# Weight conversion from a byte-shifted second load, earlier q, k and v loads, and MLP work beside the last regrouping

## Chip, cores, metric

One core of a Trainium2 chip. The metric is the device time of one execution in microseconds (us); medians of all runs of a kernel are quoted. Engines: PE is TensorE, DVE is VectorE, ACT is ScalarE, POOL is GpSimd, SP is SyncE.

## The reference, cut

```python
# q, k, v: (8, 8, 576, 64) float32; tau = 0.02
scores = np.matmul(q, k.transpose(0, 1, 3, 2)) / np.sqrt(64)
thresh = np.max(scores, axis=-1, keepdims=True) - tau
scores = np.where(scores >= thresh, scores, -1e9)
attn   = softmax(scores)                        # cut: written out in the reference
x      = (attn @ v)                             # -> (B*S, H*D) = (4608, 512)
h      = x @ w_in                               # w_in (512, 2048), float64 values
out    = (0.5 * h * (1 + erf(h / sqrt(2)))) @ w_out   # w_out (2048, 512), float64 values
```

The weights come as 64-bit floats; the kernel rebuilds 32-bit floats from their words.

## The kernel before

The attention works on 32 head pairs of 5 slots each (slot n = 5p + i). A slot computes scores, takes the softmax, and transposes the result into `pd`. Once a pair, the softmax weights are regrouped through DRAM: eight writes (`pd`), four more for the tail (`pd_tail`), two reads (`pT`). The MLP runs in the same slots from n = 24 on, filled in by `fill`. The weights come in 32 pieces of 128x512, loaded by `load_piece` and converted step by step by `conversions`, mostly before slot n = 26; that stretch is here called the front. (`sc` are the scores, `xT` the attention output before it is turned into `x`, `hT` the MLP's hidden layer.)

```python
xg = ctx.enter_context(tc.tile_pool(name="xg", bufs=6))   # weight pieces and x blocks
...
def load_piece():
    ...
    raw = xg.tile([P, 2 * PIECE], U32, tag="x", name="raw")
    nc.sync.dma_start(raw, src.bitcast(U32))
    raws.append((dst, raw))

def conversions():
    vec = nc.vector
    while raws:
        dst, raw = raws.pop(0)
        word = raw.rearrange("p (f w) -> p f w", w=2)
        lo, hi = word[:, :, 0], word[:, :, 1]
        ...
        nc.scalar.activation(low, lo, AF.Copy, bias=0.0, scale=2.0 ** -52)
        vec.tensor_scalar(cut, hi, 3, 0x3FFFFFF8, op0=ALU.logical_shift_left, op1=ALU.bitwise_and)
        yield 450
        vec.scalar_tensor_tensor(cut, hi, 0xC0000000, cut, op0=ALU.bitwise_and, op1=ALU.bitwise_or)
        yield 720
        vec.tensor_scalar(rest, hi, 27, 0xF, op0=ALU.logical_shift_right, op1=ALU.bitwise_and)
        yield 450
        vec.scalar_tensor_tensor(cut.bitcast(FP32), rest, 7.0, cut.bitcast(FP32), op0=ALU.is_ge, op1=ALU.mult)
        yield 720
        vec.tensor_scalar(two, cut, 0xFF800000, None, op0=ALU.bitwise_and)
        nc.gpsimd.tensor_tensor(low, low, two.bitcast(FP32), op=ALU.mult)
        nc.gpsimd.tensor_tensor(dst, low, cut.bitcast(FP32), op=ALU.add)
        load_piece()                  # the load three pieces on is asked for here
        converted[0] += 1
        yield 450
...
load(0, nc.scalar)
for _ in range(3):
    load_piece()
load(1)
turn_qk(0)
...
for n in range(len(slots) + WEIGH + 1):
    p, i = divmod(n, SLOTS)
    ...                               # scores, softmax, turn_p (pd at i = 4, pd_tail at i = 0)
    if i == 0 and p:
        fetch_p(p - 1)                # pT
    if i == 1 and p + 1 < NP and p:
        load(p + 1)                   # q, k: 4 DMAs each; v: 8
    if i == 2 and p + 1 < NP:
        turn_qk(p + 1)
    if n < BATCH + WEIGH:
        convert(3050)                 # so many ns of conversion steps in this slot
    elif batch < 2:
        convert(9000)
    if n > BATCH + WEIGH and batch < B:
        fill(...)                     # MLP work
    if i == WEIGH and p:
        weigh_v(p - 1)                # xT, then x
```

Nearly every DMA is issued by SyncE, in the order of the program.

## Time and profile before

| | before |
|---|---|
| median of 3 runs | 1647.19 us (1647.08 to 1648.49) |
| profiled execution | 1656.56 us, span 1654.7, mean PE clock 0.935 |
| PE, DVE, ACT, GpSimd busy, of the span | 87%, 60%, 36%, 6% |
| weight conversion on DVE, per piece | 420 + 1312 + 916 + 691 + 424 ns |
| slot n = 26 begins (PE bounds from here on) | 292.0 us |

How to read the views: a row of groups has line, engine, operation, output<-input, shape and count, then busy us and the mean ns of one, then the idle time just before them and what ended it. A row of a timeline has start, duration, engine, line and operation, and in brackets the wait. The granted clock is PE's clock as a share of full speed. In the view of groups by form of the kernel before, two conversion operations stand out:

```profile
L149 DVE SCALAR_TENSOR_TENSOR cut<-raw,cut 128x512 uint32<-128x512 uint32 x32 | 42.0, 1312 | 0.9
L152 DVE TENSOR_SCALAR rest<-raw 128x512 uint32<-128x512 uint32 x32 | 29.3, 916 | 0.0
```

The excess lies beside GpSimd's work: in the trace of the kernel before, those that overlap a GpSimd operation take 1595 and 1482 ns on average, the others 688 and 416.

### The profile page before, as it was taken

To read this page: it belongs to the slowest core of one execution; us is meant where nothing else is said; L and a number is where in the kernel's file an instruction comes from. 1 tells how busy PE (TensorE), PEld (TensorE's weight loads), DVE (VectorE), ACT (ScalarE), POOL (GpSimd) and SP (SyncE) were. 2 spreads that over 40 slices of the span, in tenths; PEclk is the share of its full clock that TensorE was granted. 3 is DMA by queue.
4 is the path that set the end of the run, shared out by engine and by line. 5 is a ranking of instruction groups with operands and counts; after the bars stand their busy time and mean duration, and the time that the engine had idled before them with its cause. 6 is when DMAs were issued, how large, how long until landed. Compare 5 with 4: busy or idle time off the path is not lost.

```text
span 1654.7 us, 17315 instructions
## 1 busy us (share of the span) xinstructions
PE 1434.5 (87%) x5888; PEld 888.9 (54%) x5888; DVE 993.3 (60%) x2176; ACT 592.0 (36%) x844; POOL 92.4 (6%) x77
## 2 busy tenths in 40 slices
PE   2334444999999999998999999999999998699999
PEld 1212223656565665656665655565657473456765
DVE  6988888776766766765766675676666675000000
ACT  3333322535354543442543344343535251101100
POOL 2232234000000000000000000000000000000000
PEclk9965556999999999999999999999999999799999
DMA  5656684576666666666576565666666665300000
GB/s 132 180 150 193 180 221 116 146 181 169 180 176 176 172 182 154 181 165 173 145 185 170 158 167 151 173 180 175 169 177 168 176 178 153 104 13 7 7 13 13
DMA packets 434982, 244.43 MB, mean 148 GB/s; under 512 B 245968, under 2 KB 418000, under 8 KB 426704
## 3 DMA queue, kind: packets, MB, share of 16 engines
q1 hardware_dynamic: 432528, 243.04, 55.9%
q8 instruction: 47, 0.77, 0.2%
q10 hardware_dynamic: 2368, 0.30, 0.1%
q14 instruction: 39, 0.32, 0.1%
HBM read 139.46 MB, written 103.81 MB: 147 GB/s over the span
## 4 chain that ended last, share of the span: by engine, by line
PE 66%; SPq 12%; DVE 12%; DMA 5%; ACT 2%; issue 2%; DVEq 0%; ACTq 0%
PE o_ps L341 27%; PE hT L330 24%; PE sc L224 9%; SPq L188 8%; PE xT L302 7%; DVE nmx L235 2%; DVE cut L149 2%; DMA turned<-pd_tail 2%; DVE p L249 2%; SPq L281 2%; SPq L277 1%; DMA k<-in_k_dram 1%; DVE rest L152 1%; DVE cut L154 1%; ACT p L236 1%
## 5 line engine op out<-in xcount | busy, mean ns | idle before, releaser
L330 PE MATMUL hT<-x,w_in 128*128 128x256 f32 x2304 | 526.0, 386 | 3.0 <-ACT x L313 3.0
L341 PE MATMUL o_ps<-w_out,g 128*128 128x512 f32 x1152 | 513.4, 597 | 0.0
L330 PEld LDWEIGHTS hT<-x,w_in 128*128 128x128 f32 x2304 | 439.4, 193 | 91.7 <-issue 26.8
L341 PEld LDWEIGHTS o_ps<-w_out,g 128*128 128x128 f32 x1152 | 214.5, 190 | 258.5 <-issue 255.4
L236 ACT ACTIVATE p<-sc,nmx 128x576 f32<-128x576 f32 x288 | 202.8, 740 | 419.6 <-DVE nmx L235 419.3
L235 DVE TENSOR_REDUCE nmx<-sc 128x1 f32<-128x576 f32 x288 | 206.1, 752 | 191.0 <-PE sc L224 190.0
L224 PE MATMUL sc<-kT,qT 64*128 64x288 f32 x1024 | 198.8, 477 | 134.9 <-DVE p L249 124.4
L224 PEld LDWEIGHTS sc<-kT,qT 64*128 64x128 f32 x1024 | 111.4, 207 | 229.9 <-issue 201.7
L249 DVE SCALAR_TENSOR_TENSOR p<-sc,thr,p 128x576 f32<-128x576 f32 x288 | 219.2, 792 | 0.3 <-ACT p L236 0.2
L302 PE MATMUL xT<-pT,v 128*64 128x288 f32 x1280 | 178.6, 434 | 34.7 <-DMA pT<-turned 20.9
L272 DVE STREAM_TRANSPOSE pd<-p 128x576 f32<-128x576 f32 x256 | 185.0, 756 | 8.9 <-DMA turned<-pd 8.9
L302 PEld LDWEIGHTS xT<-pT,v 128*64 128x64 f32 x1280 | 98.4, 145 | 117.1 <-issue 44.7
L334 ACT ACTIVATE g<-hT 128x512 f32<-128x512 f32 x144 | 84.2, 597 | 125.8 <-PE hT L330 125.0
L206 DVE STREAM_TRANSPOSE kT<-k 128x576 f32<-128x576 f32 x32 | 24.9, 778 | 167.3 <-DMA k<-in_k_dram 163.9
L260 DVE TENSOR_SCALAR p<-p,rden 128x576 f32<-128x576 f32 x252 | 121.0, 518 | 4.9
L334 ACT ACT_TABLE_LOAD x74 | 94.9, 1283 | 12.4 <-PE hT L330 11.4
L236 ACT ACT_TABLE_LOAD x73 | 93.7, 1283 | 1.3
L207 ACT ACTIVATE q<-q,q_scale 128x576 f32<-128x576 f32 x32 | 24.8, 774 | 183.8 <-DMA q<-in_q_dram 183.8
L224 PE MATMUL sc<-kT,q_tail 128*128 128x288 f32 x128 | 46.2, 490 | 43.8 <-DVE p L249 43.7
L344 ACT COPY o_sb<-o_ps 128x512 f32<-128x512 f32 x36 | 21.0, 582 | 138.8 <-PE o_ps L341 138.1
L313 ACT COPY x<-xT 128x256 f32<-128x256 f32 (+7 forms) x128 | 28.3, 288 | 90.8 <-PE xT L302 90.8
L224 PEld LDWEIGHTS sc<-kT,q_tail 128*128 128x128 f32 x128 | 25.1, 218 | 64.0 <-issue 57.2
(30 smaller groups left out, 439.9 us busy)
## 6 DMA issues: line engine op xcount, KB each, us to landing
pT<-turned SPq DMA_DIRECT2D x64, 1440.0 KB, 8.2
turned<-pd SPq DMA_DIRECT2D x256, 320.0 KB, 5.2
turned<-pd_tail SPq DMA_DIRECT2D x128, 80.0 KB, 3.0
q<-in_q_dram SPq DMA_DIRECT2D x128, 72.0 KB, 9.1
out_dram<-o_sb SPq DMA_DIRECT2D x36, 256.0 KB, 2.2
k<-in_k_dram SPq DMA_DIRECT2D x124, 72.0 KB, 3.0
raw<-in_moe_w_in_dram SPq DMA_DIRECT2D x16, 512.0 KB, 5.9
raw<-in_moe_w_out_dram SPq DMA_DIRECT2D x16, 512.0 KB, 4.4
```

The costliest lines, as they stand in the source:

```text
L149: vec.scalar_tensor_tensor(cut, hi, 0xC0000000, cut, op0=ALU.bitwise_and, op1=ALU.bitwise_or)
L188: queue.dma_start(t[e * D + f:e * D + f + Q], rows[:, :, f:f + Q])
L224: nc.tensor.matmul(sc[e][:, h, 0:HALF], lhsT=lhsT, rhs=s["kT"][rows, h * HALF:(h + 1) * HALF], start=True, stop=True)
L235: nc.vector.tensor_reduce(nmx[:, e:e + 1], sc, axis=AXIS.XY, op=ALU.max, negate=True)
L236: nc.scalar.activation(w[:, e * S:(e + 1) * S].rearrange("p (h s) -> p h s", h=2), sc, AF.Exp, bias=nmx[:, e:e + 1], scale=1.0)
L249: nc.vector.scalar_tensor_tensor(row, sc[e][:, :, 0:HALF], thr[:, e:e + 1], row, op0=ALU.is_ge, op1=ALU.mult, accum_out=den[:, e:e + 1])
L260: nc.vector.tensor_scalar(row, row, rden[:, e:e + 1], None, op0=ALU.mult)
L272: nc.vector.transpose(to[:, 0:NB, :], w[:, e * S:(e + 1) * S].rearrange("p (b i) -> p b i", i=Q))
L302: nc.tensor.matmul(xT[f, 0:HALF], lhsT=s["v"][:, e, c, :], rhs=s["pT"][e][:, c, cols], start=(c == 0), stop=(c == KR - 1))
L330: nc.tensor.matmul(hT[:, j % 2, :], lhsT=w_in_sb[c][:, j * P:(j + 1) * P], rhs=x_blk[n][:, c, :], start=(c == 0), stop=(c == N_DM - 1))
L334: nc.scalar.activation(t, hT, AF.Gelu)
L341: nc.tensor.matmul(o[:, 0:d_model], lhsT=g[j][:, m * P:(m + 1) * P], rhs=w_out_sb[j], start=(j == 0), stop=(j == N_DF - 1))
```

## The change

The intent has three parts. **Conversion:** each piece is loaded twice, the second time shifted by three bytes, so that the upper mantissa bits already lie where they are needed. Four DVE operations and one on ACT are left, and none on GpSimd. Two buffers a piece mean two pieces in flight; the new loop starts piece j+1 before it finishes piece j (`ahead`), to give ACT time. **Loads:** q, k and v are asked for two pairs ahead. **Fill:** the slots after the last pair also get MLP work.

```diff
-    xg = ctx.enter_context(tc.tile_pool(name="xg", bufs=6))
+    xg = ctx.enter_context(tc.tile_pool(name="xg", bufs=7))
...
-        raw = xg.tile([P, 2 * PIECE], U32, tag="x", name="raw")
+        raw, shifted = (xg.tile([P, 2 * PIECE], U32, tag="x", name=s) for s in ("raw", "shifted"))
         nc.sync.dma_start(raw, src.bitcast(U32))
-        raws.append((dst, raw))
+        n = 8 * PIECE - 4
+        nc.sync.dma_start(shifted.bitcast(U8)[:, 0:n], src.bitcast(U8)[:, 3:3 + n])
+        raws.append((dst, raw, shifted))
...   (the loop before, shown above, is removed; this stands in its place)
+        ahead = None
+        while raws or ahead:
+            piece = None
+            if raws:
+                dst, raw, shifted = raws.pop(0)
+                hi, top = ...
+                vec.tensor_scalar(expo, hi, 0x7FF00000, None, op0=ALU.bitwise_and)
+                nc.scalar.activation(power, expo, AF.Relu, bias=rebias, scale=8.0)
+                piece = dst, hi, top, power
+                yield 450
+            if ahead:
+                dst, hi, top, power = ahead
+                vec.tensor_scalar(mant, top, 0x0FFFFFFF, 0x10000000, op0=ALU.bitwise_and, op1=ALU.bitwise_or)
+                yield 450
+                vec.scalar_tensor_tensor(power, hi, 0x80000000, power, op0=ALU.bitwise_and, op1=ALU.bitwise_or)
+                yield 720
+                vec.scalar_tensor_tensor(dst, mant, 2.0 ** -28, power.bitcast(FP32), op0=ALU.mult, op1=ALU.mult)
+                load_piece()
+                converted[0] += 1
+                yield 720
+            ahead = piece
...
-    for _ in range(3):
+    for _ in range(2):
         load_piece()
     load(1)
     turn_qk(0)
+    load(2)
...
-        if i == 1 and p + 1 < NP and p:
-            load(p + 1)
+        if i == 1 and p + 2 < NP and p:
+            load(p + 2)
...
-            convert(3050)
+            convert(2700)
...
-        if n > BATCH + WEIGH and batch < B:
-            fill((goal[batch] - goal[batch - 1]) * BLK_NS / (BATCH if batch > 1 else BATCH - WEIGH - 1), weighed // HP)
+        if n > BATCH + WEIGH:
+            done = min(batch, B - 1)
+            fill((goal[done] - goal[done - 1]) * BLK_NS / (BATCH if done > 1 else BATCH - WEIGH - 1), weighed // HP)
```

(The rotation of v's buffers goes from 3 to 4 as well.)

More of the change, by code (lines that the diff above doesn't have):

```diff
@@ L10 @@
 U32 = mybir.dt.uint32
+U8 = mybir.dt.uint8
 AF = mybir.ActivationFunctionType
@@ L80 @@
     q_tail = [const.tile([P, P], FP32, name=f"q_tail{i}") for i in range(2)]
-    v_sb = [const.tile([P, 2, KR, D], FP32, name=f"v{i}") for i in range(3)]
+    v_sb = [const.tile([P, 2, KR, D], FP32, name=f"v{i}") for i in range(4)]
     pd = [const.tile([P, 4 * KR, P], FP32, name=f"pd{e}") for e in range(2)]
@@ L101 @@
     nc.vector.tensor_scalar(tau_eff, tau_sb, lift, None, op0=ALU.max)
+    rebias = const.tile([P, 1], FP32, name="rebias")
+    nc.vector.memset(rebias, -8.0 * 896 * 2 ** 20)
     w_in_sb = [const.tile([P, d_ff], FP32, name=f"w_in{c}") for c in range(N_DM)]
@@ L126, in load_piece @@
             return
-        raw = xg.tile([P, 2 * PIECE], U32, tag="x", name="raw")
+        raw, shifted = (xg.tile([P, 2 * PIECE], U32, tag="x", name=s) for s in ("raw", "shifted"))
         nc.sync.dma_start(raw, src.bitcast(U32))
-        raws.append((dst, raw))
+        n = 8 * PIECE - 4
+        nc.sync.dma_start(shifted.bitcast(U8)[:, 0:n], src.bitcast(U8)[:, 3:3 + n])
+        raws.append((dst, raw, shifted))
     def conversions():
         vec = nc.vector
-        while raws:
-            dst, raw = raws.pop(0)
-            word = raw.rearrange("p (f w) -> p f w", w=2)
-            lo, hi = word[:, :, 0], word[:, :, 1]
-            cut, two, rest, low = (gp.tile([P, PIECE], U32, tag="g", name=s) for s in ("cut", "two", "rest", "low"))
-            low = low.bitcast(FP32)
-            nc.scalar.activation(low, lo, AF.Copy, bias=0.0, scale=2.0 ** -52)
-            vec.tensor_scalar(cut, hi, 3, 0x3FFFFFF8, op0=ALU.logical_shift_left, op1=ALU.bitwise_and)
-            yield 450
-            vec.scalar_tensor_tensor(cut, hi, 0xC0000000, cut, op0=ALU.bitwise_and, op1=ALU.bitwise_or)
-            yield 720
-            vec.tensor_scalar(rest, hi, 27, 0xF, op0=ALU.logical_shift_right, op1=ALU.bitwise_and)
-            yield 450
-            vec.scalar_tensor_tensor(cut.bitcast(FP32), rest, 7.0, cut.bitcast(FP32), op0=ALU.is_ge, op1=ALU.mult)
-            yield 720
-            vec.tensor_scalar(two, cut, 0xFF800000, None, op0=ALU.bitwise_and)
-            nc.gpsimd.tensor_tensor(low, low, two.bitcast(FP32), op=ALU.mult)
-            nc.gpsimd.tensor_tensor(dst, low, cut.bitcast(FP32), op=ALU.add)
-            load_piece()
-            converted[0] += 1
-            yield 450
@@ new lines, in conversions @@
+        ahead = None
[3 more added lines that the diff above has]
+                dst, raw, shifted = raws.pop(0)
+                hi = raw.rearrange("p (f w) -> p f w", w=2)[:, :, 1]
+                top = shifted.rearrange("p (f w) -> p f w", w=2)[:, :, 0]
+                expo, power = (gp.tile([P, PIECE], U32, tag="g", name=s) for s in ("expo", "power"))
+                vec.tensor_scalar(expo, hi, 0x7FF00000, None, op0=ALU.bitwise_and)
[4 more added lines that the diff above has]
+                dst, hi, top, power = ahead
+                mant = gp.tile([P, PIECE], U32, tag="g", name="mant")
+                vec.tensor_scalar(mant, top, 0x0FFFFFFF, 0x10000000, op0=ALU.bitwise_and, op1=ALU.bitwise_or)
[7 more added lines that the diff above has]
+            ahead = piece
@@ L188, in load @@
                     queue.dma_start(t[e * D + f:e * D + f + Q], rows[:, :, f:f + Q])
-        t = s["v"] = v_sb[p % 3]
+        t = s["v"] = v_sb[p % 4]
         for e in range(2):
```

## The prediction

> **What bounds the kernel now.** I read the slice table first, then busy time by stage, then the timelines of SyncE, VectorE (DVE) and TensorE (PE) inside each stage. Slices of 41 us:
>
> ```profile
> PE   2334444999999999998999999999999998699999
> DVE  6988888776766766765766675676666675000000
> POOL 2232234000000000000000000000000000000000
> ```
>
> Until about 290 us DVE is the busy engine and PE is not; from there PE is, except for one dip near 1400 us. GpSimd works only in the first stage, on the weights. The same by stage (columns: busy us of PE, its loads, DVE, ACT, GpSimd; granted clock; share of the 16 DMA engines; GB/s):
>
> ```profile
> 104.00:155.50 51.50, 20.55 (x76) 11.36 (x77) 41.60 (x84) 17.69 (x29) 16.34 (x12) 0.57 0.70 193
> 292.00:1394.00 1102.00, 1079.76 (x4662) 666.19 (x4661) 743.62 (x1704) 472.69 (x653) 2.52 (x2) 0.99 0.66 170
> 1394.00:1430.00 36.00, 15.12 (x58) 6.93 (x57) 4.64 (x10) 1.88 (x6) 0.00 (x0) 0.67 0.59 164
> 1430.00:1654.70 224.70, 220.95 (x770) 145.91 (x768) 0.00 (x0) 25.68 (x43) 0.00 (x0) 1.00 0.03 11
> ```
>
> The first row is one head pair (5 slots) of the front: DVE is busy 41.6 of 51.5 us, the DMA engines 70%. The second is the middle, where PE lacks only 22 us. The third is the last regrouping, where PE idles. The fourth is MLP alone.
>
> Everything after the front is PE work in fixed order, so a front longer or shorter by X moves the end by X. What paces the front? SyncE's own timeline for one pair (pd is the regrouping write, pT its read-back):
>
> ```profile
> 102.48 10.24 SPq L277 DMA_DIRECT2D turned<-pd  x8
> 112.82 3.10 SPq L128 DMA_DIRECT2D raw<-in_moe_w_in_dram  x2
> 116.02 5.15 SPq L281 DMA_DIRECT2D turned<-pd_tail  x4
> 122.46 1.18 SPq L290 DMA_DIRECT2D pT<-turned  x2
> 124.41 6.72 SPq L188 DMA_DIRECT2D q<-in_q_dram  x4
> 131.17 4.52 SPq L188 DMA_DIRECT2D k<-in_k_dram  x4
> 135.73 5.09 SPq L194 DMA_DIRECT2D v<-in_v_dram  x8
> ```
>
> One in-order queue carries everything. Its effect on DVE in the same pair (in brackets: idle time before, and the releaser):
>
> ```profile
> 113.64 0.69 DVE L149 SCALAR_TENSOR_TENSOR cut<-raw,cut 128x512 uint32<-128x512 uint32 x1
> 119.63 0.43 DVE L147 TENSOR_SCALAR cut<-raw 128x512 uint32<-128x512 uint32 x1 [3.78 <-DMA raw<-in_moe_w_in_dram]
> 138.11 0.78 DVE L206 STREAM_TRANSPOSE kT<-k 128x576 f32<-128x576 f32 x1 [5.10 <-DMA k<-in_k_dram]
> 142.46 1.63 DVE L149 SCALAR_TENSOR_TENSOR cut<-raw,cut 128x512 uint32<-128x512 uint32 x1
> ```
>
> Three things: k, asked for one pair ahead, comes 5 us late; a weight piece queued behind pd comes 3.8 us late although it was asked for three pieces ahead; and the same operation takes 0.69 or 1.63 us. The long ones lie beside GpSimd's work.
>
> In the middle PE's gaps, added up from its timeline, are 22.0 us; at the last regrouping there is one large one:
>
> ```profile
> 1021.58 5.07 PE L302 MATMUL xT<-pT,v 128*64 128x288 f32 x20 [3.08 <-ACT g L334]
> 1418.87 1.19 PE L302 MATMUL xT<-pT,v 128*64 128x288 f32 x2 [18.84 <-DMA pT<-turned]
> ```
>
> **What the Trainium skill says.** "SBUF — State Buffer", section "Who interferes with whom": GpSimd and DVE share one pair of ports as an exclusive lock; DVE operations with two SBUF inputs or in a 2-port mode contend. The trace agrees: 1.63 against 0.69 us. "DMA: Bandwidth & Descriptors", section "Queues, rings and completion order": on each engine descriptors are consumed in ring order. The trace agrees: packets of a piece issued behind pd start only as pd's end. Same page, section "How a descriptor splits into AXI transactions": a descriptor off a 256-byte boundary starts at the boundary below. Bytes 3 to 4094 of a row then cost the same 16 transactions as the whole row, so I expect no penalty for the shift; no run shows it yet.
>
> **The change, part by part.**
>
> Conversion. Before, a piece cost DVE 420+1312+916+691+424 ns = 3.76 us (means of lines 147 to 156). After: two single-source operations (420 each, undisturbed) and two two-source ones (690 each) = 2.22 us. Over 32 pieces that is 49 us less DVE work, nearly all in the front; with 5.5 and 5.8 pieces a pair it is 20.5 against 12.8, about 8 us a pair. GpSimd's 92 us were off the path.
>
> DMA work. A raw piece is 4096 packets/32 = 128 packets of 4 KB, mean 190 ns: 1.5 us on 16 engines. The second load doubles it, 48.5 us more. A pair's other transfers come to 26.4 us (from packet durations: pd 11.2, pT 7.9, q and k 4.0, tail 2.2, v 1.1). A pair in the front then needs 26.4 + 5.8 x 3.0 = 44 us of DMA: under the present 52, so bandwidth alone does not bind.
>
> Prefetch depth. This is the decisive part, and it only shows in the order of the built program. The new loop takes up piece j+1 before it finishes piece j, and only two pieces are in flight instead of three. The first operation of piece j+2 stands directly behind the last of piece j, whose end is also where j+2's load is put in SyncE's order. Slack is zero pieces. DVE is in order, so it stops whenever SyncE has something longer ahead of that load. The seventh buffer helps only until the first x blocks take three of seven (slot 8).
>
> Walk of one pair, A = end of the second pd transpose, durations from the rows above. pd's packets end at A+14, the piece behind them lands at A+16; DVE came there at A+2: 14 us lost. Tail transposed at A+19.5, issued by A+22, landed A+24; pT read A+26 to A+34; the piece behind it A+36; DVE had come at A+22: 13 to 14 us lost. q, k, v follow (16 DMAs, at most eight outstanding), the next piece lands at A+50; DVE came at A+43: 6 us lost. Then slots of 5.0 us, piece work, 1.9 us for turning q and k: next A at A+71. The pair before x blocks exist, without the third loss: 66. The present period is 51.5. In sum: 34 lost, minus 8 and minus 5 to 9 for waits that go.
>
> Start. Loads of pair 2 (12.4 us of issue) stand ahead of the third piece, which lands near 40 us; DVE needs it at 25: first pd at 62 instead of 51. Then pd at 128, 199, 270 (before: 102, 154, 204). The last front pair converts four pieces in one slot at about 5.7 us each, because each waits a load's 4.2 us after its buffer is freed: pd at 357 instead of 267. Two pieces remain without waits, so the slot that began at 292 begins near 369: **the front gets about 77 us longer.**
>
> q, k, v ahead in the middle. The 3.08 us above is ACT sitting in order behind scaling q, whose load is late; GELU then releases PE late. Two pairs ahead removes this: I take 20 of the 22 us.
>
> MLP beside the last regrouping. Four slots of 2.08/20 block, a block being 27.6+27.5 = 55.1 us in the last stage: 22.9 us moved into a gap of 18.8+2.0 us; the products after it run at full clock (5.0 instead of 7.4 us). Saves about 24.
>
> Sum: 1647 + 77 - 20 - 24 = 1680. I take 1676, since the third loss of a pair may be smaller.
>
> **Rivals.** (a) DVE is all that counts: no load is late, the front loses 49 us of work and some 25 of waits, and the time falls to about 1647-74-44 = 1530. For it: DVE's 81%. Against: the 3.78 us wait for a piece even with three in flight. (b) DMA bandwidth binds: 44 us a pair plus queue gaps, say 48; the front gains 10 to 20 us and the time is near 1590. Against: nothing keeps the queue full if loads wait for buffers. (c) The waits for pieces come as I say but smaller, half of them: front +35, time near 1638. (d) The shifted load is slow: every landing later, over 1700.
>
> **Range and chances.** Gains of 44 in the later stages are nearly certain within 6; the front is what varies, +45 to +105. That gives 1640 to 1708. The 2% line (1680) lies in the middle of my estimate, so same and slower share the weight; faster needs the front to be no longer than before.
>
> **What would show it.** Right: VectorE's longest waits are for raw, on the first conversion operation, three a pair, 14, 14 and 6 us; pd issues at 62, 128, 199, 270, 357; conversion operations at 420 and 690 ns; middle gaps of PE under 5 us; no wait near the last xT. Wrong: pd period under 52 us, waits for raw under 10 us a pair, or packets of the shifted load well over 190 ns.

## More of the kernel before

The profiled execution was about 8 us slower than the timed ones.

DVE's longest waits in the first 300 us of the kernel before (columns: total us, times, longest us) are short for weight pieces and longer for k:

```profile
DVE kT L206 <- DMA k<-in_k_dram: 21.4, 4, 7.1
DVE cut L147 <- DMA raw<-in_moe_w_out_dram: 3.9, 1, 3.9
DVE cut L147 <- DMA raw<-in_moe_w_in_dram: 3.8, 1, 3.8
```

## The result, and the profile after

The kernel after takes **1660.59 us** (median of 4 runs, 1658.80 to 1661.91); the kernel before took 1647.84 in the same rounds. Ratios here and below are the mean time of one kernel's fast runs over the mean of the other's in the same rounds, so not quite the ratio of the medians: **1.0076, 95% interval 1.0058 to 1.0093**. That is within 2%, and the sign is clear of the noise: 12.75 us slower.

The slice table of the kernel after (slices of 41.5 us):

```profile
PE   1231313379999999999999999999999999999999
DVE  3563645677667666676776676767667676200000
POOL 0000000000000000000000000000000000000000
```

GpSimd is gone from the front and the dip of PE near the end is gone. But in the front DVE has fallen from 6 to 9 tenths to 3 to 6, and PE stays low for longer: work has been taken from the engine that was thought to pace the front, and the front is longer. By stage (columns as in the prediction: busy us of PE, its loads, DVE, ACT, POOL; granted clock; DMA share; GB/s):

```profile
128.80:196.80 68.00, 19.14 (x76) 10.76 (x76) 34.73 (x80) 18.17 (x29) 0.00 (x0) 0.58 0.64 185
...
356.50:1430.00 1073.50, 1073.50 (x4677) 659.99 (x4678) 745.33 (x1713) 475.12 (x654) 0.00 (x0) 1.00 0.67 174
1430.00:1462.70 32.70, 32.70 (x170) 26.89 (x169) 0.00 (x0) 6.97 (x13) 0.00 (x0) 1.00 0.60 170
```

The pair that took 51.5 us takes 68.0, with DVE busy for 34.7 of them and the DMA engines at 64%: neither is full. The middle has no gap in PE at all, at full clock, and the last regrouping has none either. DVE's longest waits in the first 360 us of the kernel after name what the front waits for:

```profile
DVE expo L154 <- DMA raw<-in_moe_w_in_dram: 78.1, 9, 16.0
DVE expo L154 <- DMA raw<-in_moe_w_out_dram: 64.4, 10, 13.0
```

142.5 us of waiting for weight pieces, where the kernel before has 7.7. The conversion itself is as cheap as planned (groups by form of the kernel after):

```profile
L154 DVE TENSOR_SCALAR expo<-raw 128x512 uint32<-128x512 uint32 x32 | 13.5, 422 | 142.6 <-DMA raw<-in_moe_w_in_dram 78.1 <-DMA raw<-in_moe_w_out_dram 64.4
L161 DVE TENSOR_SCALAR mant<-shifted 128x512 uint32<-128x512 uint32 x32 | 13.4, 420 | 0.1
L163 DVE SCALAR_TENSOR_TENSOR power<-raw,power 128x512 uint32<-128x512 uint32 x32 | 21.9, 683 | 0.0
```

Why the pieces are late is seen when SyncE's timeline and DVE's are laid side by side, for the same pair of the kernel after. First SyncE, what it issues in order:

```profile
128.84 10.57 SPq L285 DMA_DIRECT2D turned<-pd  x8
139.51 1.18 SPq L132 DMA_DIRECT2D raw<-in_moe_w_in_dram  x1
...
148.65 2.60 SPq L289 DMA_DIRECT2D turned<-pd_tail  x4
151.65 1.69 SPq L298 DMA_DIRECT2D pT<-turned  x2
153.38 0.52 SPq L132 DMA_DIRECT2D raw<-in_moe_w_in_dram  x1
...
154.57 8.73 SPq L196 DMA_DIRECT2D q<-in_q_dram  x4
163.35 3.74 SPq L196 DMA_DIRECT2D k<-in_k_dram  x4
167.13 5.09 SPq L202 DMA_DIRECT2D v<-in_v_dram  x8
172.33 0.52 SPq L132 DMA_DIRECT2D raw<-in_moe_w_in_dram  x1
```

Then DVE, first the start of the kernel and then the pair:

```profile
40.90 0.43 DVE L154 TENSOR_SCALAR expo<-raw 128x512 uint32<-128x512 uint32 x1 [16.01 <-DMA raw<-in_moe_w_in_dram]
...
145.55 0.43 DVE L154 TENSOR_SCALAR expo<-raw 128x512 uint32<-128x512 uint32 x1 [13.28 <-DMA raw<-in_moe_w_in_dram]
163.77 0.43 DVE L154 TENSOR_SCALAR expo<-raw 128x512 uint32<-128x512 uint32 x1 [12.01 <-DMA raw<-in_moe_w_in_dram]
176.29 0.43 DVE L154 TENSOR_SCALAR expo<-raw 128x512 uint32<-128x512 uint32 x1 [5.79 <-DMA raw<-in_moe_w_in_dram]
```

Each single weight load stands behind one long group (pd; the tail and pT; q, k, v), and the DVE operation that uses it stands directly behind the operation after which it was asked for. So DVE idles three times a pair: 13.3, 12.0 and 5.8 us. The order acts in two places. Behind pd, 7.2 of the 13.3 us pass before SyncE comes to the load (DVE has idled since 132.3, the load is issued at 139.5). Behind pT the load is issued 1.6 us after DVE stops, at 153.4, but its packets start only at 160.4, when pT's are nearly through. Of the third wait only 1.8 us lie before the issue; the other 4 are the load itself.

| | before | predicted | after |
|---|---|---|---|
| pd issued, pairs 0 to 4 (us) | 51.0, 102.5, 154.0, 204.4, 267.2 | 62, 128, 199, 270, 357 | 64.7, 128.8, 196.8, 264.6, 342.9 |
| slot n = 26 begins | 292.0 | 369 | 356.5 |
| from n = 26 to the end, profiled | 1362.7 | 1362.7 - 44 | 1302.8 |
| PE's gaps in the middle | 22.0 | 2 | 0 |

The front is 64.5 us longer, the rest 59.9 us shorter. In the profiles that is +4.6; the timed runs say +12.75, because the profiled execution of the kernel before was some 8 us slower than its timed ones.

### The profile page after: what moved, and what is told of

It reads as the page before. It is cut to its first block, busy times and chain, and to the rows that moved or that the text cites. A ratio compares the mean times of both kernels' runs of the same rounds, so it can differ in the third digit from the quotient of the medians.

```text
span 1659.3 us, 17059 instructions
## 1 busy us (share of the span) xinstructions
PE 1408.2 (85%) x5888; PEld 872.8 (53%) x5888; DVE 936.4 (56%) x2145; ACT 596.9 (36%) x844; POOL 3.5 (0%) x14
## 4 chain that ended last, share of the span: by engine, by line
PE 79%; SPq 8%; DVE 6%; DMA 5%; issue 1%; ACT 1%; ACTq 0%
PE hT L338 31%; PE o_ps L349 30%; PE sc L232 10%; PE xT L310 8%; SPq L196 3%; SPq L285 2%; DMA raw<-in_moe_w_in_dram 2%; DMA raw<-in_moe_w_out_dram 2%; SPq L202 2%; DVE nmx L243 1%; DVE p L257 1%; DMA q<-in_q_dram 1%; DMA turned<-pd_tail 1%; DVE pd L280 1%; DVE power L163 1%
## 5 line engine op out<-in xcount | busy, mean ns | idle before, releaser
L338 PE MATMUL hT<-x,w_in 128*128 128x256 f32 x2304 | 520.1, 383 | 14.9 <-ACT x L321 14.9
L338 PEld LDWEIGHTS hT<-x,w_in 128*128 128x128 f32 x2304 | 435.0, 191 | 101.5 <-issue 27.5
L232 PE MATMUL sc<-kT,qT 64*128 64x288 f32 x1024 | 195.2, 473 | 216.2 <-DVE p L257 205.9
L310 PE MATMUL xT<-pT,v 128*64 128x288 f32 x1280 | 167.2, 417 | 0.0
L310 PEld LDWEIGHTS xT<-pT,v 128*64 128x64 f32 x1280 | 91.0, 140 | 78.7 <-issue 18.0
L154 DVE TENSOR_SCALAR expo<-raw 128x512 uint32<-128x512 uint32 x32 | 13.5, 422 | 142.6 <-DMA raw<-in_moe_w_in_dram 78.1
L155 ACT ACTIVATE power<-expo,rebias 128x512 uint32<-128x512 uint32 x32 | 23.0, 719 | 183.6 <-DVE expo L154 183.6
L232 PE MATMUL sc<-kT,q_tail 128*128 128x288 f32 x128 | 41.8, 452 | 16.2 <-DVE p L257 16.2
L266 ACT ACTIVATE p<-p,rden 128x576 f32<-128x576 f32 x36 | 26.2, 768 | 46.9 <-DVE rden L262 46.9
```

What stands on the lines that cost most here:

```text
L232: nc.tensor.matmul(sc[e][:, h, 0:HALF], lhsT=lhsT, rhs=s["kT"][rows, h * HALF:(h + 1) * HALF], start=True, stop=True)
L310: nc.tensor.matmul(xT[f, 0:HALF], lhsT=s["v"][:, e, c, :], rhs=s["pT"][e][:, c, cols], start=(c == 0), stop=(c == KR - 1))
L338: nc.tensor.matmul(hT[:, j % 2, :], lhsT=w_in_sb[c][:, j * P:(j + 1) * P], rhs=x_blk[n][:, c, :], start=(c == 0), stop=(c == N_DM - 1))
```

## The experiments

Theory **A**, that of the prediction: the front is longer because a weight load has no slack. It is asked for one piece ahead (two in flight, one already taken up) in a queue where much longer things stand before it. Rival **B**: the other parts (q, k, v two pairs ahead) crowd the front. Rival **C**: the second load's traffic, or its odd offset, makes the DMA system slow. Rival **D**: the new conversion is not cheaper in practice, because of its dependence on ACT.

Differences against the kernel after are taken across rounds and chips; the median of the kernel before moved between 1647.8 and 1652.3 us in them, so a few us of such a difference mean nothing.

### One part alone: e1, e2, e3, and two together: e4

e1 is the kernel after with loads and fill put back; e2, e3 and e4 are the kernel before with parts added.

```diff
 # e1, from the kernel after (v's buffers and the fill's lines put back as well)
-    load(2)
-        if i == 1 and p + 2 < NP and p:
-            load(p + 2)
+        if i == 1 and p + 1 < NP and p:
+            load(p + 1)
 # e2, from the kernel before (v's buffers 3 -> 4 as well)
+    load(2)
-        if i == 1 and p + 1 < NP and p:
-            load(p + 1)
+        if i == 1 and p + 2 < NP and p:
+            load(p + 2)
 # e3, from the kernel before
-        if n > BATCH + WEIGH and batch < B:
+        if n > BATCH + WEIGH:
             ...   # the fill's lines of the change
 # e4: e2 and e3
```

> The new conversion alone (byte-shifted second load, seven buffers, two pieces in flight), with q, k, v one pair ahead and no MLP beside the last regrouping, as before. Theory A (a piece's load has no slack behind the regrouping on the one queue): the front grows by 45 to 65 us (waits for raw of about 14 and 12 us a pair stay; the 16 us wait at the start shrinks, since no loads of pair 2 stand ahead), the gaps in the middle and the 19 us gap at the end stay: 1690 to 1715 us. Rival B (the loads two pairs ahead lengthen the front, the conversion is as good as its instruction times): below 1647, about 1610.

> The old conversion with three pieces in flight, only q, k, v two pairs ahead. Theory A: the 5 us waits for k in the front go (15 to 20 us), the 22 us of gaps in the middle go and with them the half-clock stretches (10 to 13 us more in the profile): 1597 to 1615 us. Rival B: the front grows by 20 us or more, so 1640 or above.

> Only MLP work beside the last regrouping. Both theories: the 18.8 us wait for pT at the end goes and the stretch at half clock with it: 1621 to 1627 us, 22.9 us of MLP less behind it.

> The old conversion with both other parts. Theory A: the two gains add up, 1573 to 1592 us, so the new conversion costs the whole change 70 to 85 us. Rival B: near 1620.

| run | median us (before on that chip: 1652.29) | ratio | n = 26 begins |
|---|---|---|---|
| e1 conversion alone | 1699.26 | 1.0285 [1.0268, 1.0303] | 347.7 |
| e2 loads alone | 1608.71 | 0.9739 [0.9725, 0.9754] | 276.5 |
| e3 fill alone | 1627.65 | 0.9859 [0.9841, 0.9877] | about 290 |
| e4 loads and fill | 1584.09 | 0.9590 [0.9576, 0.9605] | 277.0 |

The conversion alone costs 47 us, the loads alone save 44, the fill alone saves 25. Loads and fill add up (e4: 68). All four came as expected (under theory A where the theories differ), but for e3, 0.65 us above its range. e2's stretch from 300 to 1330 us, with the old conversion, shows that the clean middle comes from the loads:

```profile
300.00:1330.00 1030.00, 1029.77 (x4481) 632.69 (x4478) 713.39 (x1639) 456.98 (x629) 0.00 (x0) 1.00 0.68 176
```

In e3 the wait before the last products is 0.82 instead of 18.84 us (its PE timeline):

```profile
1417.90 5.06 PE L302 MATMUL xT<-pT,v 128*64 128x288 f32 x38 [0.82 <-DMA pT<-turned]
```

The conversion does not add up with the others: 47 - 44 - 25 would be -22, and the change gave +13, so about 34 us are lost in the combination. Rival B is right to that extent. Two terms are seen. First, at the start the third piece waits behind the loads of pair 2, 16.0 us against 6.5 in e1 (e1's DVE timeline):

```profile
31.60 0.43 DVE L154 TENSOR_SCALAR expo<-raw 128x512 uint32<-128x512 uint32 x1 [6.53 <-DMA raw<-in_moe_w_in_dram]
```

Second, the 15.5 us by which e2 shortens the front (292.0 to 276.5) can't be had when DVE waits for pieces anyway: in e1, with q, k and v one pair ahead as before, DVE does not wait for k in the front at all (its only wait for k, 5.0 us, comes at 365 us, after the front), where in the kernel before it waits 21.4 us. The two come to 25 us, and the front shows 24: 292.0 + 55.7 - 15.5 would be 332.2, and it is 356.5. Another 7 us of the later stages' gain was already there in e1 (1355.3 from n = 26 to the end, against 1362.7). Most of that need not be the conversion's: from n = 26 to the last pd issue, e3, which runs the code of before there, is also 4.6 us shorter than the profile of the kernel before.

### Slack: e5 and e9, kernels that compute the right result

e5 takes a piece up only after the one before it is finished; the load of piece j+2 then has the whole of piece j+1 as slack. e9 keeps the early take, with eight buffers, and loads the unshifted row one piece earlier than the shifted one.

```diff
 # e5, from the kernel after: the body of the loop without `ahead`
+        while raws:
+            dst, raw, shifted = raws.pop(0)
+            ...   # expo, Relu on ACT, mant, power, dst of the same piece, one after the other
+            load_piece()
 # e9, from the kernel after
-    xg = ctx.enter_context(tc.tile_pool(name="xg", bufs=7))
+    xg = ctx.enter_context(tc.tile_pool(name="xg", bufs=8))
     # load_piece() loads raw alone; load_shifted() loads the shifted row of the oldest piece without one
+                load_shifted()
                 load_piece()
     # start: two pieces with both loads, then
+    load_piece()
```

> The changed kernel, all three parts, same loads and buffers, but a piece is finished before the next is taken up, so two pieces in flight give one piece of slack; VectorE then waits for ScalarE's half about 0.5 us in each piece. Theory A (no slack behind the regrouping on one queue): the waits for raw fall from about 32 us a pair to 12 to 16, the 16 us wait at the start to under 10; 1590 to 1615 us. Theory C (the cost is the doubled traffic of the weights): unchanged or slightly worse, 1660 to 1675.

> A correct kernel with all three parts and eight buffers: the plain load of a piece is asked for one piece earlier than its shifted load, so that each has one piece of slack with the early take kept. Theory A: waits for raw 10 to 15 us a pair, no wait for ScalarE: 1580 to 1605 us. Theory C: 1655 to 1665.

e5 took 1620.31 us (0.9815 [0.9792, 0.9838]), 40 us less than the kernel after; waits for pieces fell from 142.5 to 90.5 us (73.4 for the plain row, 17.1 for the shifted one), n = 26 began near 315. Waiting for ACT, the reason for the early take, cost DVE 10 us. e9 took 1618.83 (0.9807 [0.9789, 0.9825]), with 100.5 us of waits, of them 17.3 at the start. Both missed their expectation, by 5 and 14 us: in pair 1, one piece of slack took some 5, 5 and 2 us off the three waits, which is less than pd's or pT's group lasts, so 8, 7 and 4 us stay in e5 (waits for both rows). A's direction is borne out; the gain from one piece of slack was overestimated.

### Traffic against slack: e6, e7, e11, wrong results on purpose

Here the shifted load is left out and the same tile is read twice. The numbers are wrong (relative error 0.50), the instructions on DVE and ACT are the same. With one buffer a piece, the number in flight can be varied.

```diff
-        raw, shifted = (xg.tile(...) for s in ("raw", "shifted"))
+        raw = shifted = xg.tile([P, 2 * PIECE], U32, tag="x", name="raw")
-        nc.sync.dma_start(shifted.bitcast(U8)[:, 0:n], src.bitcast(U8)[:, 3:3 + n])
-    for _ in range(2):
+    for _ in range(2):      # e6;  range(3) in e7;  range(4) in e11
```

> Wrong on purpose: the shifted load is left out and the mantissa is taken from the unshifted piece, so the weights' traffic is that of before; two pieces in flight with the early take, no slack. Theory A: the waits behind pd, pT and q, k, v stay, each 1 to 2 us shorter: 1635 to 1655 us. Theory C: the cost goes, 1575 to 1590 us.

> Wrong on purpose: as the run with the unshifted piece alone, but three pieces in flight, so one piece of slack. Theory A: waits for raw fall to about 10 us a pair, 1570 to 1590 us. Theory C: the same time as with two in flight.

> Wrong on purpose: no shifted load, four pieces in flight, so two pieces of slack as in the old conversion. What the cheaper instructions and the idle GpSimd are worth when no piece comes late: VectorE has 8 us less a pair than in the run of both other parts with the old conversion (1584 us). Theory A: 1545 to 1570 us. If something else on the queue sets the front: 1575 to 1590.

| run | in flight | waits for pieces, us | median us | ratio |
|---|---|---|---|---|
| after | 2, two loads each | 142.5 | 1660.6 | 1.0076 |
| e6 | 2 | 117.9 | 1636.58 | 0.9916 [0.9897, 0.9934] |
| e7 | 3 | 68.3 | 1587.67 | 0.9619 [0.9600, 0.9638] |
| e11 | 4 | 26.6 | 1550.41 | 0.9401 [0.9387, 0.9415] |

Taking the shifted loads away, which is half of the weights' traffic, issues and buffers, saves 24 us; each further piece in flight then saves 49 and 37 us at the same traffic. The wait follows the number in flight. So C has a share of 24 us, the smaller one, and it is not the odd offset: in the trace of the kernel after, packets of the shifted load took 172.6 ns on average (4092 bytes), those of the plain one 199.6 (4096 bytes; 189.6 before). What is left of the waits in e11 (DVE's waits, first 360 us) is less than a fifth of that in the kernel after:

```profile
DVE expo L152 <- DMA raw<-in_moe_w_out_dram: 14.6, 4, 4.2
DVE expo L152 <- DMA raw<-in_moe_w_in_dram: 12.0, 5, 5.1
```

e11 is also what decides D: with little late, the new conversion is worth 34 us against the old one in e4 (1550.4 against 1584.1). It is cheaper, as the prediction's arithmetic said; it could not show that while pieces came late. (e11 also loads half as much as a right kernel must.)

### The old conversion without slack: e10

e4 with `range(1)`: one piece in flight, plain loads, old conversion.

```diff
-    for _ in range(3):
+    for _ in range(1):
         load_piece()
```

> The old conversion with the two other parts (1584 us) and one piece in flight instead of three: the next piece is asked for only when it is needed, so no slack, with old instructions and old traffic. Theory A: the same three waits a pair as in the changed kernel, the front 45 to 75 us longer: 1630 to 1660 us. If the slack matters only together with the shifted load: below 1600.

It took 1703.25 us (1.0326 [1.0310, 1.0342]), 119 us more than e4, with 144.4 us of waits for pieces and n = 26 at 395.9. The expectation was missed by 43 us. What A says of the sign holds even with the old conversion: no slack alone is enough to undo everything. The size shows that with no slack a piece's DVE work adds to the load instead of hiding it: against e6, which has the same traffic and no slack either, its five pd issues lie 8 to 43 us later (66.95 to 362.07 against 58.71 to 319.18), 5 to 14 us more a pair. That this is due to the longer operations alone is argued, not shown: e10 has no early take, and one piece in flight where e6 has two.

### Another queue: e8, e12

The weight loads, and only they, are issued by ACT (e8) or GpSimd (e12), so that they no longer stand in SyncE's order.

```diff
-        nc.sync.dma_start(raw, src.bitcast(U32))
+        nc.gpsimd.dma_start(raw, src.bitcast(U32))        # e12;  nc.scalar in e8
-        nc.sync.dma_start(shifted.bitcast(U8)[:, 0:n], src.bitcast(U8)[:, 3:3 + n])
+        nc.gpsimd.dma_start(shifted.bitcast(U8)[:, 0:n], src.bitcast(U8)[:, 3:3 + n])
```

> The changed kernel with both loads of every weight piece issued by ScalarE instead of SyncE, so that they don't stand behind pd, pT and q, k, v in SyncE's order. Slack is still zero. Theory A (order on the one queue is most of the cost): waits for raw fall from 32 us a pair to about 20, mostly the bare 4 us of a load, and the 16 us wait at the start goes: 1600 to 1635 us. If only the missing slack counts and not what stands ahead: 1650 or more.

> The changed kernel with both loads of every weight piece issued by GpSimd, which has nothing else to do and issues as soon as a buffer is free, not when ScalarE or SyncE come to it. Theory A: no wait at the start, waits for raw at or below those of the run on ScalarE's queue: 1590 to 1630 us. If only the slack counts: 1650 or more.

e8 took 1607.84 us (0.9748 [0.9732, 0.9764]), e12 1580.11 (0.9579 [0.9562, 0.9595]): 53 and 80 us less than the kernel after, with the same bytes, the same slack in the program and the same operations. e12 was better than expected. ACT has its own work in order, so its issues are late too (82.2 us of waits for pieces); GpSimd has nothing else to do. In e12 the waits fell to 50.7 us (groups by form):

```profile
L154 DVE TENSOR_SCALAR expo<-raw 128x512 uint32<-128x512 uint32 x32 | 13.4, 421 | 50.7 <-DMA raw<-in_moe_w_out_dram 40.1 <-DMA raw<-in_moe_w_in_dram 10.6
```

The operation takes 421 ns as before: issuing from GpSimd did not slow it down. This settles A's main point: the same loads in a queue where nothing long stands before them are not late by 13 us. It also refutes C as the main cause, since the bytes are all still moved. Whether the gain comes from the earlier issue or from packets that no longer wait behind pd's and pT's is not told apart here: the new queue changes both.

### Both: e13, e14

e13 is e9, e14 is e5, each with the loads on GpSimd's queue (the edit of e12).

> The staggered kernel (one piece of slack, eight buffers) with the weights' loads issued by GpSimd. If slack and order are two terms: waits for raw under 5 us a pair, the front near that of the run with four unshifted pieces in flight: 1545 to 1562 us. If the doubled traffic or VectorE sets the front: 1570 to 1582, no better than GpSimd's queue alone.

> The kernel without the early take with the weights' loads issued by GpSimd. Two terms: 1550 to 1570 us, up to 10 us more than the staggered one for the waits on ScalarE. One term: 1570 to 1585.

e13 took **1555.63 us** (0.9430 [0.9407, 0.9452]), e14 1565.27 (0.9489 [0.9468, 0.9511]); both compute the right result and beat both kernels. In e13 the waits for pieces are 9.6 us in all (groups by form, first 260 us):

```profile
L163 DVE TENSOR_SCALAR expo<-raw 128x512 uint32<-128x512 uint32 x32 | 13.3, 419 | 9.6 <-DMA raw<-in_moe_w_out_dram 6.7 <-DMA raw<-in_moe_w_in_dram 2.9
```

and its slices show the front at last as the change meant it to be, with DVE at 6 to 9 tenths from the start and PE full from the seventh slice (38.8 us each) on:

```profile
PE   2344539999999999999999999999999999999999
...
DVE  6777978777777666666666767677766676000000
```

In e14 DVE waits 15.2 us for ACT, and e14 is 9.6 us slower than e13. That the early take is worth this is likely but not shown: e13 also has an eighth buffer and staggered loads. What DVE waits for in e13's first 400 us is now PE (41.0 us) and its own pd writes (26.6 us). n = 26 began near 249 in e13, 107 us earlier than in the kernel after, and 105 us of time are gained: the front is all of it.

## Why the prediction was right or wrong, point by point

**Right: what the front waits for, and where.** Three waits a pair, behind pd, behind pT, behind q, k and v, forecast as 14, 14 and 6 us, measured as 13.3, 12.0 and 5.8. The pd times lie within 3 us for the first three pairs. e12 shows the order of the queue to be the cause, e7 and e11 the missing slack.

**Right: no penalty for the shift**, 172.6 ns a packet, as the page cited in the prediction let one expect. **Right: the operations**, 422, 420, 683 and 690 ns. **Right: no wait near the last xT.** PE's timeline of the kernel after, where before there were 18.84 us of idle time:

```profile
1429.86 22.18 PE L338 MATMUL hT<-x,w_in 128*128 128x256 f32 x102
1451.96 5.07 PE L310 MATMUL xT<-pT,v 128*64 128x288 f32 x40
```

**Wrong in size: the front, +77 forecast, +64.5 measured.** The step that failed is "the last front pair converts four pieces in one slot at about 5.7 us each, because each waits a load's 4.2 us": the pair took 78.3 us instead of 87, which is 8.7 of the 12.5 us. A piece there took 4.7 us (three of them in the 14.0 us from 326.8 to 340.8), because each waited 2.2 to 3.3 us for its load and not 3.5 (5.7 less 2.2 of work); that is 4 us. The loss behind pd in that pair was 8.1 us instead of 14, which is 6 more. The other pairs took 64.1, 68.0 and 67.8 instead of 66, 71 and 71, because the second loss was 12 and not 13 to 14; the start was late by 2.7 us more than forecast, and the stretch from the last pd to n = 26 took 13.6 us instead of 12.

**Wrong in size: the later stages, -44 forecast, -59.9 measured (in profiles).** The step that failed is the sum "-20 - 24": it took the gaps of PE in the middle as their whole cost. The granted clock was in the sum at the end (5.0 instead of 7.4 us) but not in the middle. Two windows of the kernel before around one gap of 3.08 us show it (the gap, then the products after it; the clock is the third number from the end):

```profile
1018.50:1021.58 3.08, 0.00 (x1) 0.00 (x0) 3.04 (x7) 3.05 (x5) 0.00 (x0) 0.86 0.29 108
1021.58:1026.00 4.42, 4.42 (x20) 2.18 (x20) 1.60 (x6) 0.79 (x3) 0.00 (x0) 0.50 0.00 0
```

The 20 products after the gap ran at half clock and took 5.07 us (PE's timeline, shown in the prediction); 20 of the same kind just before it took 2.65. The clock record of the trace has four such stretches in the middle, beginning within 3.3 us of the start of gaps of 2.18, 5.52, 3.65 and 3.08 us. They last 3.4, 6.8, 3.4 and 6.8 us, and PE is busy in 16.9 us of these; one more covers the first 5.1 us from n = 26. The kernel after has none from n = 26 on. Half of 16.9 + 5.1 is 11.0 us. With all 22 us of the gaps and the 24 of the end, the sum is 57 us; the last 3 of the 59.9 are not accounted for. The Trainium skill has this effect: "TensorE: Matmul & The Clock Gate", section "What's actually happening", has the array fall to half clock after an idle window of about 3.4 us and come back after as long a busy one. The stretches here, 3.4 or 6.8 us long, are one or two such windows; the gaps that set them off were in part shorter (last section). The prediction had not drawn on it. The runs agree that gap and half clock go together: after the first few us from n = 26, e2 has half clock at the last regrouping only (23.9 us), e3 in the middle only (13.7), e4 none.

**The total.** 77 - 44 = +33 was the sum of the steps; the prediction took 4 off for a smaller third loss, so +29. +12.75 was measured. Both errors lower the result, together by 28 us, to the +4.6 that the two profiles show. The timed runs show 8 us more than that, because the profiled execution of the kernel before was slow; so some of the 59.9 us belongs to that execution and not to the change. Where it lies can be seen against e3, whose code is that of the kernel before up to the last regrouping: e3's profile issues its last pd at 1390.2 us, that of the kernel before at 1396.6. Of these 6.5 us some 2 are in the front, 2.5 are PE's gaps in the middle (22.2 against 19.7) and 2 are half clock behind them. So these losses vary from one execution to the next, and part of the -59.9 is the chance of which execution was profiled. The range held. Of the rivals, (a) and (b) are refuted by 142.5 us of waits with DVE at half load and the DMA engines at 64%; (d) by the packets; (c), "as I say but smaller", came nearest in time, though the waits were nearly whole and not half.

**Open.** Why the gaps in the middle differ between executions of the same code; the timed runs give only a mean clock, 0.936 to 0.940 in the other executions of the kernel before against 0.935 in the profiled one. Whether the old conversion would gain as much in GpSimd's queue. How e10's excess divides.

## What to carry to other kernels

Count a prefetch in pieces between the point where a load enters its queue and the first instruction that needs it, in the order of the built program, and compare that time with the longest group that may stand in the queue before it: a loop that takes the next piece up early spends a buffer's worth of slack. When a change makes the work cheaper and the loads more, move the loads to a queue of their own before judging it; here the new conversion alone cost 47 us in the shared queue, and in a queue of its own, staggered, it is part of the fastest correct kernel, 28 us under the best with the old one (1555.6 against 1584.1; the old conversion was not tried in that queue). A gap of PE can cost more than its length (here 3.08 us of gap were followed by 20 products at 5.07 instead of 2.65 us), so look at the granted clock behind each gap.

## What the Trainium skill lacked or had wrong

- "TensorE: Matmul & The Clock Gate": section "What's actually happening" gives one idle window of about 3.4 us as the condition for half clock, and section "Why this matters for your kernels" advises against gaps over about 3 us. In the kernel before, a gap of 2.18 us was followed by 3.4 us at half clock, and in e1 gaps of 2.12 and 2.20 us by 3.4 us each; in e3 a gap of 2.59 us was followed by none, nor were gaps of 1.88 us and less in the kernel before. About 2 us is the safer limit here.
- "DMA: Bandwidth & Descriptors", section "Issuing engines are not separate DMA queues": it says that issuing from several engines saves only the issue time, which is usually small. Moving only the weight loads to GpSimd's queue took 80 us from this kernel (1660.6 to 1580.1), because a load then no longer stands behind groups whose issue waits for earlier transfers. The passage lacks this case, of one late stream in a shared order.
- The page cited in the prediction gives the transactions of a descriptor off a 256-byte boundary, but no page has a measured time for one. Here a load whose source is off by three bytes took 172.6 ns a packet of 4092 bytes, against 199.6 for packets of 4096 aligned bytes in the same run: no price was seen.
